# A list scheduler's latency table: result latency between dependent operations of one engine, and extra latency into TensorE

## The chip, the cores and the metric

The kernel runs on one core of one Trainium2 chip. The metric is the device time of one execution in microseconds (us); smaller is better. The times shown are those of three plain runs, and one more execution was taken with the hardware profiler. TensorE is called PE, VectorE DVE, ScalarE ACT, GpSimd POOL, and SP is the engine that issues the DMAs.

## The reference

Four layers follow one another on x (2048 tokens of 512 values, bf16): attention with a carried memory, a gated feed-forward network (FFN), the same attention again, the same FFN again. Each is added to its input, and each works on the layer-normalised input. Attention walks over 64 segments of 32 tokens; each segment needs the memory that the one before left:

```python
for s in range(n_seg):                                   # 64 segments of 32 tokens
    h = jnp.concatenate([mem, xs], axis=1)               # 8 memory rows + 32 tokens = 40 rows
    q, k, v = (jnp.einsum('btd,dhe->bhte', h, W) for W in (Wq, Wk, Wv))   # 32 heads of 128
    scores = jnp.where(mask, jnp.einsum('bhqe,bhke->bhqk', q, k) * scale, -1e9)
    o = jnp.einsum('bhqk,bhke->bhqe', softmax(scores), v)
    o = jnp.einsum('bhte,hed->btd', o, Wo)
    mem = o[:, :M, :]                                    # the memory of the next segment
    outs.append(o[:, M:, :])
# FFN:
h = sigmoid(x @ w_gate) * (x @ w_up)                     # 512 -> 1792
y = h @ w_down                                           # 1792 -> 512
```

## The kernel before

**Steps.** The two attention layers run interleaved. Step t (0 to 69) works on segment t of the first layer and, from step 6, on segment t-6 of the second ("both" steps, 6 to 63, have 80 columns, 40 of each). After every fourth step one FFN block of 128 tokens of each layer becomes possible. The serial path is the memory: the output projection of step t must be complete, over all 32 heads, before the first q/k matmul of step t+1.

**One step** (`emit_step`) takes the heads in six groups, five of six heads and a last one of two; they are called groups 0 to 5 here. For each group PE computes q and k in two units of three heads (L385, into one of three PSUM tiles `pj`), ACT copies them to `qku` (L599), and PE computes the scores (L403) into the one PSUM tile `s_ps`. The softmax is a chain of small operations on 104x240 values: DVE adds the mask (L410, `st<-s_ps,maskb`), takes the maximum (L413, `mx`), subtracts it (L415), ACT takes the exponential (L418), DVE sums (L420, `sm`), takes the reciprocal (L422, `rs`) and multiplies twice, once for each layer (L426, `pb`). PE transposes the result (L436, `pt_ps`), ACT or DVE copies it (`ptsb`, L599 or L601), PE multiplies with v (L461, `ot_ps`; v itself comes from L451 and ACT's copy `vsb`), ACT copies (`otsb`), and PE adds the output projection into `wo_ps` (L477). At the end of a step DVE copies the new memory from `wo_ps` into the next step's `hT` (L488).

**The FFN** of a block (`ffn`) uses one PSUM tile, `misc_ps`, for everything: transposes (L510, L324), seven pairs of gate and up products (L535; ACT's tanh L542 and DVE's L544 follow each pair), and fourteen matmuls down (L556). The layer norms (L312 to L318) are chains of four small DVE operations, one POOL operation and one ACT operation.

**What sets the order.** Every piece of work is entered as a `Task` with an engine, a duration in ns and the tiles it reads (`r`) and writes (`w`). `Planner.plan` then runs a list schedule over all tasks of the program: each task has a `tail`, the longest path of durations and latencies to the end; whenever an engine comes free, it takes the ready task with the longest tail. The engines' instruction streams are written in that order, and on the chip every engine works its stream in order. So the table `LAT` never appears as an instruction; it only decides the order. Two successors are told apart: between tasks of one engine the latency is 0, otherwise it is that of the earlier task's engine. The tasks for `ptsb` and for part of `hT` may go to ACT or DVE, whichever the planner finds free first.

Of the kernel before, what the change touches and what calls it, by code (L numbers as in the profile page):

```python
# [12 lines left out]
ALU = mybir.AluOpType  # L13
# [10 lines left out]
EPS = 1e-5  # L24
# [18 lines left out]
class Task:  # L43
    __slots__ = ("eng", "dur", "lat", "fn", "deps", "succ", "tail", "boost", "ndep", "ready", "start", "idx", "on")

    def __init__(self, eng, dur, lat, fn, boost):
        self.eng, self.dur, self.lat, self.fn, self.boost = eng, dur, lat, fn, boost
        self.deps, self.succ = set(), []


class Planner:

    LAT = {"PE": 215.0, "DVE": 130.0, "ACT": 140.0, "POOL": 450.0, "SP": 2200.0}

# [5 lines left out]
    def add(self, eng, dur, fn, r=(), w=(), lat=None, boost=0.0):  # L62
        engs = eng if isinstance(eng, tuple) else (eng,)
        tk = Task(engs, dur, self.LAT[engs[0]] if lat is None else lat, fn, boost)
        tk.idx = len(self.tasks)
        for k in r:
            if k in self.writer:
                tk.deps.add(self.writer[k])
        for k in w:
            if k in self.writer:  # L70
                tk.deps.add(self.writer[k])
            for q in self.readers.get(k, ()):
                tk.deps.add(q)
# [7 lines left out]
        return tk  # L81

    def plan(self):
        T = self.tasks
# [17 lines left out]
        ready = {e: [] for e in free}  # L102
# [11 lines left out]
        while left:  # L114
            best = None
            for e in free:
# [5 lines left out]
                if h:  # L122
                    t = free[e]
# [6 lines left out]
            t, e = best  # L130
# [24 lines left out]
class Kern:  # L155
# [149 lines left out]
    def layernorm_T(self, xb, xkey):  # L305
# [6 lines left out]
        pl.add("DVE", dve_ns(D), lambda: nc.vector.bn_stats(out=ln[:, 0:6], in_=xb), r=[xkey], w=[lk])  # L312
        pl.add("DVE", 100, lambda: nc.vector.bn_aggr(out=ln[:, 6:8], in_=ln[:, 0:6]), w=[lk])
        pl.add("DVE", 80, lambda: nc.vector.tensor_scalar(out=ln[:, 8:9], in0=ln[:, 7:8], scalar1=EPS, scalar2=None, op0=ALU.add), w=[lk])
        pl.add("POOL", 500, lambda: nc.gpsimd.tensor_tensor(out=ln[:, 9:10], in0=ln[:, 8:9], in1=self.negh[:], op=ALU.pow), w=[lk], lat=100)
        pl.add("DVE", 80, lambda: nc.vector.scalar_tensor_tensor(out=ln[:, 10:11], in0=ln[:, 6:7], scalar=-1.0, in1=ln[:, 9:10],
                                                                  op0=ALU.mult, op1=ALU.mult), w=[lk])
        pl.add("ACT", act_ns(D) + 180, lambda: nc.scalar.activation(out=xn[:], in_=xb, func=ACTF.Identity, bias=ln[:, 10:11], scale=ln[:, 9:10]),  # L318
# [27 lines left out]
    def emit_step(self, t):  # L346
# [21 lines left out]
        for g, (h0, gsz, us) in enumerate(self.groups):  # L368
            hs = slice(0, gsz)
            for u in us:  # L370
# [29 lines left out]
                def sc(uh=uh, nh=nh, qku=qku, h0=h0):  # L400
# [19 lines left out]
            pl.add("DVE", dve_ns(n), lambda hs=hs, st=st, sm=sm: nc.vector.tensor_reduce(out=sm[pr, hs], in_=st[pr, hs], axis=AX.X, op=ALU.add),  # L420
# [238 lines left out]
```

## Time and profile before

| | |
|---|---|
| median of the three runs | 2194.81 us (2194.67 to 2200.37) |
| the profiled execution's own time | 2198.24 us |
| its span, first to last instruction | 2196.4 us |
| PE busy | 2056.8 us, 42116 matmuls |
| ACT busy | 1299.0 us |
| DVE busy | 1270.8 us |
| granted PE clock, mean | 0.987 |

A page of the profile gives busy times, a chain of waits followed back from the last instruction, groups of instructions, and DMA issues. A row of a timeline reads: start, duration, engine, line, operation, output<-inputs, how many were merged, and in brackets how long the engine sat idle before it and for whom. A row of a windows view gives, for a stretch of time, its length and the busy time and instruction count of PE, PE's weight loads (PEld), DVE, ACT and POOL, then the granted PE clock, the busy share of the DMA engines and their GB/s. A matmul's recorded duration includes the time in the pipeline, so matmuls overlap in the records; what a matmul costs PE is the distance from one start to the next, and the rows of the chain of waits give just that.

### The profile page before, as it was taken

The numbers are of one execution on the slowest core, as the hardware profiler recorded it, in microseconds if no ns is written. First come the engines' busy times: TensorE is split into PE (matmuls) and PEld (weight loads), VectorE is DVE, ScalarE is ACT, GpSimd is POOL, SyncE is SP. The second block draws the span as 40 slices with busy tenths as digits, with TensorE's granted clock in tenths as the row PEclk, the third lists the DMA queues.
The fourth block names the chain that finished last, engine by engine and source line by source line (L and its number), as shares of the span: only waits on it lengthen the run. The fifth ranks groups of instructions, "written<-read, shape, count | busy, mean of one in ns | idle before, by whom it ended". The sixth has DMA issues, their size and how long they took to land.

```text
span 2196.4 us, 93329 instructions
## 1 busy us (share of the span) xinstructions
PE 2056.8 (94%) x42116; PEld 1742.8 (79%) x42116; DVE 1270.8 (58%) x3743; ACT 1299.0 (59%) x2919; POOL 43.5 (2%) x77
## 2 busy tenths in 40 slices
PE   4999999999999999999999999999999999999996
PEld 3777878788887878888787778878787888878775
DVE  4566566556646655665566466556655655565653
ACT  3556566565656656565666556566665666666552
POOL 1000000000000000000000000000000000000000
PEclk8999999999999999999999999999999999999997
DMA  9030223233232323324132332423233242324223
GB/s 333 29 89 17 77 60 108 74 108 103 75 108 60 108 74 108 103 75 122 55 113 60 108 103 74 119 58 109 63 113 98 83 116 60 115 58 126 70 61 107
DMA packets 317330, 203.17 MB, mean 92 GB/s; under 512 B 11770, under 2 KB 316930, under 8 KB 316930
## 3 DMA queue, kind: packets, MB, share of 16 engines
q1 hardware_dynamic: 316930, 197.19, 30.7%
q8 instruction: 329, 5.39, 1.0%
q14 instruction: 71, 0.58, 0.1%
HBM read 195.04 MB, written 2.10 MB: 90 GB/s over the span
## 4 chain that ended last, share of the span: by engine, by line
PE 62%; DVE 29%; issue 3%; ACT 3%; DMA 2%; POOL 0%; DVEq 0%; POOLq 0%; ACTq 0%
PE pj L385 22%; PE pj L451 16%; PE misc_ps L535 7%; PE wo_ps L477 7%; DVE pb L426 7%; DVE st L410 4%; DVE mx L413 3%; DVE st L415 3%; DVE sm L420 3%; PE misc_ps L556 3%; PE s_ps L403 3%; DVE ptsb L601 2%; DMA wd<-in_B_w_down_dram 2%; PE ot_ps L461 2%; PE pt_ps L436 2%
## 5 line engine op out<-in xcount | busy, mean ns | idle before, releaser
L385 PE MATMUL pj<-hT,wq_sb 128*128 128x80 bf16 (+1 forms) x8960 | 626.4, 198 | 16.1 <-DVE hT L488 13.6
L385 PE MATMUL pj<-hT,wk_sb 128*128 128x80 bf16 (+1 forms) x8960 | 627.6, 198 | 0.0
L451 PE MATMUL pj<-wv_sb,hT 128*104 128x512 bf16 x2240 | 568.3, 384 | 1.8 <-ACT vsb L599 1.6
L385 PEld LDWEIGHTS <-wq_sb 128*128 128x128 bf16 x8960 | 465.2, 99 | 59.6 <-issue 21.7
L599 ACT CAST qku<-pj 128x480 bf16<-128x480 f32 (+3 forms) x770 | 389.4, 514 | 144.4 <-PE pj L385 103.9
L599 ACT CAST vsb<-pj 104x512 bf16<-104x512 f32 (+2 forms) x560 | 326.1, 585 | 229.4 <-PE pj L451 223.4
L385 PEld LDWEIGHTS <-wk_sb 128*128 128x128 bf16 x8960 | 451.1, 99 | 0.0
L477 PE MATMUL wo_ps<-otsb,wo_sb 128*128 128x80 bf16 (+1 forms) x8960 | 389.3, 198 | 4.6 <-ACT otsb L599 4.2
L477 PEld LDWEIGHTS <-wo_sb 128*128 128x128 bf16 x8960 | 351.2, 99 | 40.7 <-issue 9.3
L451 PEld LDWEIGHTS <-hT 128*104 128x104 bf16 x2240 | 253.3, 128 | 128.1 <-issue 5.1
L410 DVE TENSOR_TENSOR st<-s_ps,maskb 104x240 f32<-104x240 f32 (+5 forms) x420 | 158.0, 376 | 296.7 <-PE s_ps L403 290.0
L426 DVE TENSOR_TENSOR pb<-st,rs 64x240 bf16<-64x240 f32 (+3 forms) x768 | 287.9, 375 | 26.7 <-DVE rs L422 0.5
L418 ACT ACTIVATE st<-st 104x240 f32<-104x240 f32 (+5 forms) x420 | 161.2, 384 | 188.2 <-DVE st L415 185.7
L599 ACT CAST otsb<-ot_ps 128x480 bf16<-128x480 f32 (+3 forms) x420 | 204.4, 487 | 66.6 <-PE ot_ps L461 60.4
L403 PEld LDWEIGHTS <-qku 128*128 128x128 bf16 x4096 | 173.1, 96 | 78.6 <-issue 34.5
L403 PE MATMUL s_ps<-qku 128*128 128x40 bf16 x4096 | 201.6, 180 | 24.5 <-DVE st L410 21.7
L544 DVE SCALAR_TENSOR_TENSOR hff<-th,misc_ps 128x256 bf16<-128x256 f32 x224 | 93.4, 417 | 210.6 <-ACT th L542 208.9
L420 DVE TENSOR_REDUCE sm<-st 104x6 f32<-104x240 f32 (+5 forms) x420 | 155.8, 371 | 95.7 <-ACT st L418 92.9
L535 PE MATMUL misc_ps<-xnT,wg 128*128 128x128 bf16 x1792 | 176.3, 222 | 9.5 <-DVE hff L544 6.6
L535 PE MATMUL misc_ps<-xnT,wu 128*128 128x128 bf16 x1792 | 176.6, 222 | 0.0
L436 PE MATMUL pt_ps<-ident,pb 128*128 128x80 bf16 (+1 forms) x2240 | 145.4, 198 | 32.8 <-DVE pb L426 27.8
L413 DVE TENSOR_REDUCE mx<-st 104x6 f32<-104x240 f32 (+5 forms) x420 | 156.9, 374 | 13.5
(52 smaller groups left out, 1671.3 us busy)
## 6 DMA issues: line engine op xcount, KB each, us to landing
wg<-in_B_w_gate_dram SPq DMA_DIRECT2D x224, 256.0 KB, 3.1
wu<-in_B_w_up_dram SPq DMA_DIRECT2D x224, 256.0 KB, 3.5
wd<-in_B_w_down_dram SPq DMA_DIRECT2D x224, 256.0 KB, 2.9
wv_sb<-in_A_Wv_dram SPq DMA_DIRECT2D x8, 512.0 KB, 9.6
wo_sb<-in_A_Wo_dram SPq DMA_DIRECT2D x8, 512.0 KB, 8.1
wq_sb<-in_A_Wq_dram SPq DMA_DIRECT2D x5, 768.0 KB, 10.3
wk_sb<-in_A_Wk_dram SPq DMA_DIRECT2D x5, 768.0 KB, 11.1
xs<-in_A_x_dram SPq DMA_DIRECT2D x16, 128.0 KB, 2.1
```

What stands on the lines that cost most here:

```text
L385: nc.tensor.matmul(o_ap, lhsT=W[:, c, h * P:(h + 1) * P], rhs=mv(c), start=(c == 0), stop=(c == DC - 1))
L403: nc.tensor.matmul(s_all[:, uh - h0 + i, :], lhsT=qku[:, i, j, :], rhs=qku[:, i, 2 + j, JOFF * j:JOFF * j + L], start=(idx == 0), stop=(id ...
L410: pl.add("DVE", dve_ns(n, True), lambda gsz=gsz, hs=hs, st=st: nc.vector.tensor_tensor(out=st[pr, hs], in0=s_all[pr, hs], in1=self.maskb[p ...
L413: pl.add("DVE", dve_ns(n), lambda hs=hs, st=st, mx=mx: nc.vector.tensor_reduce(out=mx[pr, hs], in_=st[pr, hs], axis=AX.X, op=ALU.max), r=[ ...
L418: pl.add("ACT", act_ns(n), lambda hs=hs, st=st: nc.scalar.activation(out=st[pr, hs], in_=st[pr, hs], func=ACTF.Exp, scale=self.scale), w=[ ...
L420: pl.add("DVE", dve_ns(n), lambda hs=hs, st=st, sm=sm: nc.vector.tensor_reduce(out=sm[pr, hs], in_=st[pr, hs], axis=AX.X, op=ALU.add), r=[ ...
L426: pl.add("DVE", dve_ns(n), lambda gsz=gsz, hs=hs, st=st, rs=rs, pb=pb, pj_=pj_, npj_=npj_, j=j: nc.vector.tensor_tensor(out=pb[pj_, hs, JO ...
L436: nc.tensor.matmul(o_ap, lhsT=pb[:, hl, :], rhs=idn, start=True, stop=True)
L451: nc.tensor.matmul(pv[0:LW, :], lhsT=hT[:, c, :], rhs=self.wv[:, c, n0 * P:(n0 + 4) * P], start=(c == 0), stop=(c == DC - 1))
L477: nc.tensor.matmul(self.wo_ps[:, c * ncol:(c + 1) * ncol], lhsT=self.wo[:, h, c * P:(c + 1) * P], rhs=otsb[:, hl, 0:ncol], start=(h == 0 a ...
L535: nc.tensor.matmul(gu[:, 2 * i + k, :], lhsT=W[:, c, i * P:(i + 1) * P], rhs=xnT[:, c, :], start=(c == 0), stop=(c == DC - 1))
L599: nc.scalar.copy(out=dst, in_=src)
```

## The change

It touches only what the planner believes. Four things are altered:

- `LAT` gets new values, and 45 ns (`TO_PE`) are added wherever the later task is on PE.
- A task now keeps, in `fresh`, those of its dependences that it reads (not those it only overwrites). Between two tasks of DVE, or two of ACT, a `fresh` dependence now costs the latency of the table; it cost 0.
- To make such reads visible, the layer norm's and softmax's in-place tasks now name in `r` the tile that they read.
- The POOL task `pow` is entered with 520 ns and the table's 100 ns, where it had 500 and an explicit 100.

```diff
-    LAT = {"PE": 215.0, "DVE": 130.0, "ACT": 140.0, "POOL": 450.0, "SP": 2200.0}
+    LAT = {"PE": 205.0, "DVE": 122.0, "ACT": 130.0, "POOL": 100.0, "SP": 2200.0}
+    TO_PE = 45.0
...
         for k in r:
             if k in self.writer:
                 tk.deps.add(self.writer[k])
+                tk.fresh.add(self.writer[k])
...
+    def gap(self, a, b):
+
+        if a.eng == b.eng:
+            return a.lat if a.idx in b.fresh and a.eng[0] in ("DVE", "ACT") else 0.0
+        return a.lat + (self.TO_PE if b.eng[0] == "PE" else 0.0)
...
             for s in tk.succ:
-                same = T[s].eng == tk.eng
-                m = max(m, T[s].tail + (0.0 if same else tk.lat))
+                m = max(m, T[s].tail + self.gap(tk, T[s]))
...
                 n = T[s]
-                same = n.eng == (e,)
-                n.ready = max(n.ready, t + tk.dur + (0.0 if same else tk.lat))
+                n.ready = max(n.ready, t + tk.dur + self.gap(tk, n))
...
-        pl.add("DVE", 100, lambda: nc.vector.bn_aggr(out=ln[:, 6:8], in_=ln[:, 0:6]), w=[lk])
+        pl.add("DVE", 100, lambda: nc.vector.bn_aggr(out=ln[:, 6:8], in_=ln[:, 0:6]), r=[lk], w=[lk])
...
                 out=st[pr, hs], in0=st[pr, hs], in1=mx[pr, hs].unsqueeze(2).to_broadcast([npart, gsz, L]), op=ALU.subtract),
-                r=[("mx", gi)], w=[("st", gi)])
+                r=[("mx", gi), ("st", gi)], w=[("st", gi)])
             pl.add("ACT", act_ns(n), lambda hs=hs, st=st: nc.scalar.activation(out=st[pr, hs], in_=st[pr, hs], func=ACTF.Exp, scale=self.scale),
-                   w=[("st", gi)])
+                   r=[("st", gi)], w=[("st", gi)])
```

No instruction is added, removed or altered in itself; PE has the same 42116 matmuls. The order of nearly every engine's stream changes somewhere, and 41 of the 420 copies to `ptsb` go from DVE to ACT (170 on DVE before, 129 now). The line numbers of the changed kernel are larger by 6 from `Kern` on: L410 is L416 there, L601 is L607, and so on.

The first place is DVE's stream in the middle of step 30. Before, from the mask addition of group 2 (`st_77<-s_ps`) to that of group 3 (`st_78<-s_ps`):

```order
L410 TENSOR_TENSOR st_77<-s_ps,maskb 104x240
L413 TENSOR_REDUCE mx_81<-st_77 104x6
L415 TENSOR_TENSOR st_77<-st_77,mx_81 104x240
L420 TENSOR_REDUCE sm_84<-st_78 104x6
L422 RECIPROCAL rs_86<-sm_84 104x6
L426 TENSOR_TENSOR pb_80<-st_78,rs_86 64x6x40
L426 TENSOR_TENSOR pb_80<-st_78,rs_86 40x6x40
L420 TENSOR_REDUCE sm_83<-st_77 104x6
L422 RECIPROCAL rs_85<-sm_83 104x6
L426 TENSOR_TENSOR pb_79<-st_77,rs_85 64x6x40
L426 TENSOR_TENSOR pb_79<-st_77,rs_85 40x6x40
L410 TENSOR_TENSOR st_78<-s_ps,maskb 104x240
```

The same place in the changed kernel (`st_77` is again group 2, `st_78` first group 1 and, from its next mask addition on, group 3):

```order
L416 TENSOR_TENSOR st_77<-s_ps,maskb 104x240
L428 RECIPROCAL rs_86<-sm_84 104x6
L607 CAST ptsb_87<-pt_ps 128x480
L419 TENSOR_REDUCE mx_81<-st_77 104x6
L432 TENSOR_TENSOR pb_80<-st_78,rs_86 64x6x40
L421 TENSOR_TENSOR st_77<-st_77,mx_81 104x240
L432 TENSOR_TENSOR pb_80<-st_78,rs_86 40x6x40
L426 TENSOR_REDUCE sm_83<-st_77 104x6
L416 TENSOR_TENSOR st_78<-s_ps,maskb 104x240
L428 RECIPROCAL rs_85<-sm_83 104x6
L522 TENSOR_TENSOR xa_99<-misc_ps,xs_93 128x512
L419 TENSOR_REDUCE mx_82<-st_78 104x6
```

Before, an operation was followed by the one that reads its result nearly everywhere; now operations of two groups alternate, and the mask addition of group 3 stands ahead of group 2's reciprocal and multiplications, where it stood behind them. Over the whole program, 1787 neighbouring pairs of DVE's stream were dependent ones, and 1109 are now.

The second place is PE's stream at the end of step 28: the last output projections and what follows them. Before:

```order
L477 LDWEIGHTS wo_sb
L477 MATMUL wo_ps<-otsb_91,wo_sb 128x80
L477 LDWEIGHTS wo_sb
L477 MATMUL wo_ps<-otsb_91,wo_sb 128x80
L385 LDWEIGHTS wq_sb
L385 MATMUL pj_128<-hT_70,wq_sb 128x80
```

At the same six positions now:

```order
L541 LDWEIGHTS wu_114
L541 MATMUL misc_ps<-xnT_107,wu_114 128x128
L541 LDWEIGHTS wu_114
L541 MATMUL misc_ps<-xnT_107,wu_114 128x128
L391 LDWEIGHTS wq_sb
L391 MATMUL pj_128<-hT_70,wq_sb 128x80
```

Eight matmuls of the FFN (four of `wg`, four of `wu`) now stand between the last projection of the step and the first q/k matmul of the next; they stood ahead of that projection. In steps 8 to 61 the order repeats every four steps. Of four step ends there, one had an FFN piece at this position before (two matmuls of L556), and three have now: eight matmuls after step 28, sixteen after step 30, and the two of L556 after step 31, as before. Step 29 has none.

A third displacement is on PE between score pieces. Before, scores of a group's two units had up to a q/k piece between them; now they are mostly neighbours. From the last score matmul of group 3 to the first of group 4 there stood, in steps 28 to 31, pieces of 0.65 to 0.88 us; now there stand pieces of 1.08 to 1.52 us, worked out from the row counts and the distance of starts of each shape in the trace of before.

More of the change, by code (lines that the diff above doesn't have):

```diff
@@ L43 @@
 class Task:
-    __slots__ = ("eng", "dur", "lat", "fn", "deps", "succ", "tail", "boost", "ndep", "ready", "start", "idx", "on")
+    __slots__ = ("eng", "dur", "lat", "fn", "deps", "succ", "tail", "boost", "ndep", "ready", "start", "idx", "on", "fresh")
     def __init__(self, eng, dur, lat, fn, boost):
         self.eng, self.dur, self.lat, self.fn, self.boost = eng, dur, lat, fn, boost
-        self.deps, self.succ = set(), []
+        self.deps, self.succ, self.fresh = set(), [], set()
 class Planner:
-    LAT = {"PE": 215.0, "DVE": 130.0, "ACT": 140.0, "POOL": 450.0, "SP": 2200.0}
+    LAT = {"PE": 205.0, "DVE": 122.0, "ACT": 130.0, "POOL": 100.0, "SP": 2200.0}
+    TO_PE = 45.0
     def __init__(self):
```

6 lines of the change are left out of this document (3 added, 3 removed).

## The prediction

> **What bounds the kernel now.** I read the page first: its engine shares and the chain that ended last.
>
> ```profile
> span 2196.4 us, 93329 instructions
> PE 2056.8 (94%) x42116; PEld 1742.8 (79%) x42116; DVE 1270.8 (58%) x3743; ACT 1299.0 (59%) x2919; POOL 43.5 (2%) x77
> PE 62%; DVE 29%; issue 3%; ACT 3%; DMA 2%; POOL 0%; DVEq 0%; POOLq 0%; ACTq 0%
> ```
>
> PE is busy nearly all the time, yet 29% of the chain is DVE, which is busy only 58%. So DVE decides in certain places. A table of stages shows where; the row of 126.60 us is one repeat of four steps (28 to 31), the last row is the crowded middle of step 30.
>
> ```profile
> 0.00:57.00 57.00, 28.46 (x524) 21.90 (x525) 22.56 (x62) 18.28 (x44) 9.47 (x15) 0.83 1.04 332
> 230.00:1949.00 1719.00, 1645.38 (x33110) 1405.45 (x33110) 1016.74 (x2981) 1044.94 (x2281) 29.11 (x53) 1.00 0.32 91
> 2134.00:2196.40 62.40, 45.90 (x712) 34.47 (x709) 19.81 (x56) 18.94 (x49) 0.55 (x1) 0.74 0.40 116
> 866.40:993.00 126.60, 121.73 (x2454) 104.03 (x2452) 75.32 (x221) 77.20 (x169) 2.20 (x4) 1.00 0.32 92
> 944.00:954.00 10.00, 8.94 (x167) 7.17 (x165) 9.34 (x29) 7.66 (x16) 0.55 (x1) 1.00 0.01 2
> ```
>
> The steady part is 1719 us, so it matters most; it is 13.6 repeats of 126.6 us, of which steps 8 to 61 are 13.5. In the crowded middle DVE is at 93% and ACT at 77%: there DVE is the bound.
>
> What PE must do in four steps follows from the code's counts and the distance of starts, which the chain of waits gives (start, us, engine, output, line, count):
>
> ```profile
> 869.66 0.86 PE pj L385 x24
> 889.48 1.73 PE pj L451 x8
> 882.49 0.31 PE s_ps L403 x12
> 891.21 0.86 PE wo_ps L477 x24
> 893.03 0.45 PE misc_ps L535 x8
> 892.16 0.22 PE pt_ps L436 x6
> 868.36 0.43 PE misc_ps L556 x2
> 876.39 0.22 PE misc_ps L324 x4
> ```
>
> 1024 q/k matmuls cost 36.7 us, 128 of v 27.7, 256 scores 6.6, 512 projections 18.3, 224 gate/up 12.6, 256 transposes and products with v 9.4, 28 down 6.0, 24 of the norms 1.3: together 118.6 us. So **PE loses 8.0 of 126.6 us** in each repeat, and no order can gain more than about 13.5 x 8.0 = 108 us there. PE's waits in this window name most of it (us in total, times, longest):
>
> ```profile
> PE s_ps L403 <- DVE st L410: 1.5, 2, 1.1
> PE pj L385 <- DVE hT L488: 0.9, 3, 0.3
> PE misc_ps L324 <- ACT xn L318: 0.9, 1, 0.9
> PE pt_ps L436 <- DVE pb L426: 0.8, 2, 0.6
> ```
>
> They show less than is lost, because each matmul's record runs on in the pipeline. Step 30 shows how much: six matmuls from 945.91 would let the next start at 946.12; it starts at 947.35, so 1.23 us are lost where the bracket says 1.06.
>
> ```profile
> 945.17 0.46 PE L403 MATMUL s_ps<-qku 128*128 128x40 bf16 x12
> 945.91 0.38 PE L461 MATMUL ot_ps<-ptsb,vsb 128*128 128x80 bf16 x6
> 947.35 0.30 PE L403 MATMUL s_ps<-qku 128*128 128x40 bf16 x6 [1.06 <-DVE st L410]
> ```
>
> The cause is on DVE:
>
> ```profile
> 942.60 0.40 DVE L410 TENSOR_TENSOR st<-s_ps,maskb 104x240 f32<-104x240 f32 x1
> 943.03 0.40 DVE L413 TENSOR_REDUCE mx<-st 104x6 f32<-104x240 f32 x1
> 943.47 0.41 DVE L415 TENSOR_TENSOR st<-st,mx 104x240 f32<-104x240 f32 x1
> 943.80 0.40 DVE L420 TENSOR_REDUCE sm<-st 104x6 f32<-104x240 f32 x1
> 944.23 0.19 DVE L422 RECIPROCAL rs<-sm 104x6 f32<-104x6 f32 x1
> 945.30 0.40 DVE L420 TENSOR_REDUCE sm<-st 104x6 f32<-104x240 f32 x1
> 945.74 0.19 DVE L422 RECIPROCAL rs<-sm 104x6 f32<-104x6 f32 x1
> 946.04 0.82 DVE L426 TENSOR_TENSOR pb<-st,rs 64x240 bf16<-64x240 f32 x2
> 946.89 0.41 DVE L410 TENSOR_TENSOR st<-s_ps,maskb 104x240 f32<-104x240 f32 x1
> 947.21 0.41 DVE L516 TENSOR_TENSOR xa<-misc_ps,xs 128x512 bf16<-128x512 bf16 x1
> ```
>
> Group 3's scores are done at 945.48, but its mask addition (946.89) stands in the queue behind group 2's sum, reciprocal and multiplications. And the distances of starts tell the price that the old table left out: an operation that reads its forerunner's result starts 0.43 to 0.44 us after it (942.60, 943.03, 943.47; 943.80 to 944.23), one that doesn't 0.32 to 0.33 (943.47 to 943.80; 946.89 to 947.21). The **0.11 us** between them is what the new 122 ns stands for. The old plan believed each softmax chain some 0.5 us shorter than it is, so PE's pieces were put where their inputs aren't ready.
>
> The Trainium skill speaks against this gain: "VectorE: DVE Perf Modes", section "The DRAIN you can't avoid", says that the next DVE operation starts only when the pipe is empty, whether or not a semaphore stands between, so that independent neighbours would save nothing. The trace decides otherwise here, by 0.32 against 0.44 us; the same section allows an earlier start for an operation that isn't held.
>
> **The change part by part**, per repeat of four steps. No instruction's duration changes; each term is a wait.
>
> (a) *Step ends.* Today three of the four step ends cost PE 0.48 us each:
>
> ```profile
> 959.40 0.45 PE L477 MATMUL wo_ps<-otsb,wo_sb 128*128 128x80 bf16 x8
> 960.17 0.30 PE L385 MATMUL pj<-hT,wq_sb 128*128 128x80 bf16 x4 [0.31 <-DVE hT L488]
> ```
>
> (eight projections from 959.40 end at 959.69; 960.17 is 0.48 later.) The new order puts 0.45 us of FFN into one of them and 0.90 into another. Saved: 0.45 + 0.48 = **0.9 us**. Bounds: 0, if these FFN pieces themselves wait for `misc_ps`, to 1.4.
>
> (b) *Scores waiting for `s_ps`.* Over the program the page names 21.7 us:
>
> ```profile
> L403 PE MATMUL s_ps<-qku 128*128 128x40 bf16 x4096 | 201.6, 180 | 24.5 <-DVE st L410 21.7
> ```
>
> In the repeat it is the 1.5 us of the row above, 0.17 more for each of its two waits, and 0.4 in two waits too short to open a gap between records (counted from starts): 2.2 us, all before group 4's scores. Now 1.1 to 1.5 us of PE work stands there in place of 0.65 to 0.88, and in step 30 the mask addition stands ahead of the three operations that it waited for, which took 945.74 to 946.86. The piece needs group 3's scores, DVE free, and 0.46 us (946.89 to 947.35). I expect 0.3 us to be left and take **1.9**. Bounds: 0.8 (group 3's addition late in every step as today's step 30) to 2.2.
>
> (c) *Transposes waiting for `pb`.* Today 1.65 us: 0.8 in the row, 0.17 for each of its two, and 0.5 in short ones. For groups 0 to 4 the work between scores and transposes is now 4.8 to 8.6 us, and the chain takes 4 to 5.5 when I lay step 30's new DVE order on the distances above. For the small group 5 only 3.2 to 3.5 us stand there, and in steps 29 and 30 layer-norm operations cut in: some 0.4 and 0.7 us of wait. Saved: **0.4**. Bounds: -1.0 to 1.65.
>
> (d) *The second layer's norm in step 29.*
>
> ```profile
> 921.11 0.60 PE L556 MATMUL misc_ps<-wd,hff 128*128 128x512 bf16 x2
> 926.56 0.40 PE L324 MATMUL misc_ps<-ident,xn 128*128 128x128 bf16 x4 [0.88 <-ACT xn L318]
> ```
>
> From the last down product (end 921.55) to the transposes it takes 5.0 us, with 4.0 us of PE work between; now 4.4 us stands there. That is 1.05 us (0.88 and the hidden 0.17); the next transposes wait 0.3. Of these 1.35 I take 0.8 as left: **0.55** saved. Bounds: 0 to 1.35.
>
> (e) *Small waits* on `ptsb`, `otsb` and `hff`, 1.2 us together (8.0 less 1.4, 2.2, 1.65, 1.35 and 0.2 of DMA). In step 29 the last projection now follows its own product with v at once, which costs some 0.5; others go. Saved: **0.35**. Bounds: -0.6 to 1.2.
>
> The sum is 0.9 + 1.9 + 0.4 + 0.55 + 0.35 = 4.1 us per repeat, half of what is lost; 13.5 repeats give **55 us**. Outside them I take nothing: the first 57 us wait for weights (DMA share 1.04) and PE's clock (0.83); the last 62 are the last FFN block alone, whose order is the same. In steps 0 to 7 and 62 to 69 five step ends lose the FFN piece that they had (5 x 0.45 = 2.2 us), against smaller waits in the other terms; bounds -5 to +10 us. The profiled execution took 2198.24 us, 1.8 more than its span; 2198.2 - 55 = 2143, and it lay 3.4 us above the runs' median of 2194.81, so I predict **2139 us**.
>
> **The rivals.**
>
> *Only PE's own distances help.* What stands against my walk through DVE is that a chain cut by other operations gets longer: each inserted operation costs 0.32 where it saves 0.11. Term (a) stays 0.9. Term (b), with group 3 ready as late as today (1.0 to 1.9 us after its scores; 945.48 to 947.35 is the longest) against 1.1 to 1.5 us of work now, leaves 0.7: 1.5 saved. The transposes of group 3 come 5.1 to 6.2 us after its scores today, against 4.8 to 5.7 us of work now, and lose 0.6; the rest stays. 1.8 us per repeat, 24 in all: 2171 us. By the rule of the Trainium skill weighed above this would be the outcome; the 0.11 us of this trace speak against it.
>
> *The waits only move.* Every wait removed from `s_ps` comes back at transposes and norms; (b) and (c) at their lower ends, (d) 0, (e) -0.6, (a) 0.45: 0.35 us lost per repeat, 5 us in all: 2200 us, inside what is called no change below.
>
> *ACT becomes the late engine: slower.*
>
> ```profile
> L599 ACT CAST ptsb<-pt_ps 128x480 bf16<-128x480 f32 (+2 forms) x250 | 117.1, 469 | 70.6 <-PE pt_ps L436 67.2 <-DVE st L410 1.3 <-DVE sm L420 0.4
> ```
>
> 41 such copies move to ACT, three net in each repeat, and they gather in the crowded middle: in step 28 groups 1, 2 and 3 change from DVE to ACT. ACT is at 77% there, so about five more copies of 0.47 us fill the ten us; from that point the `qku` copies behind them are late, `pj` stays full, and PE waits. Two such waits of 0.47 in each step cost 3.8 us per repeat; with only (a) gained that is 2.9 x 13.5 = 39 us slower: 2234 us. Against it: at most three more per step, and the exponentials beside them come earlier.
>
> **How the numbers follow.** Chances: forecast 0.70 (2105 to 2160), distances only 0.14, moved waits 0.07, ACT late 0.09. With every term at its upper end, 8.0 less 0.2 of DMA waits is gone, about 100 us; I don't believe that of step 29, whose end has no piece and whose last projection waits (1.0 us stays), and with half a microsecond left in each of the other steps it is 6.3 x 13.5 = 85 us: 2110. The range reaches from a little below that, 2108, to 2186, past the first rival; it leaves out the two last rivals and a little at the lower end. A measurement of this kernel tells 0.3% (6.6 us) from no change: faster by more 0.84, within 0.07, slower by more 0.09.
>
> **What would show it.** In the profile after: a repeat of about 122.5 us with the same 118.6 of PE work; three PE waits on `hT` per repeat gone down to one; the wait of `s_ps` on L416 down from 21.7 us over the program to below 6; `pt_ps` on `pb` little smaller. Wrong would be a growing wait of `qku` or `pj` on ACT, FFN pieces at the step ends that wait for `hff`, or neighbours on DVE that start 0.44 us apart though independent.

## The result and the profile after

| | before | after |
|---|---|---|
| median of four runs each, side by side on one chip | 2194.74 us (2193.3 to 2200.37) | 2104.16 us (2100.89 to 2105.69) |
| the profiled execution | 2198.24 us | 2105.36 us |

The ratio is 0.9581 with a 95% interval of 0.956 to 0.9602: the changed kernel is 90.6 us (4.2%) faster. The forecast was 55 us, to 2139. The direction holds, and so does the mechanism at the step ends and the scores; the size doesn't, and the time lies 4 us below the range's lower end.

The page of the changed kernel, with the lines that were read first in the one of before (span, busy times, shares of the chain that ended last):

```profile
span 2103.6 us, 93419 instructions
PE 2021.3 (96%) x42006; PEld 1735.4 (82%) x42116; DVE 1197.1 (57%) x3702; ACT 1304.5 (62%) x2960; POOL 43.8 (2%) x77
PE 82%; DVE 10%; ACT 3%; issue 2%; DMA 1%; another core or an unknown queue 0%; POOL 0%; ACTq 0%; SPq 0%; POOLq 0%; DVEq 0%
```

DVE's part of the chain falls from 29% to 10%, though its share of busy time only goes from 58 to 57%: DVE holds PE back in far fewer places. (110 records of L562's matmuls are missing, 42006 for 42116, so PE's busy time and counts are a little low here; starts and spans are not touched by that.)

The stages of the changed kernel, at the same points of the program as the table in the prediction (stretch, length, busy time and count of PE, PEld, DVE, ACT and POOL, granted clock, DMA share, GB/s):

```profile
0.00:57.00 57.00, 28.06 (x495) 21.18 (x496) 22.84 (x62) 18.45 (x44) 9.52 (x15) 0.82 1.04 332
223.00:1863.00 1640.00, 1615.62 (x33009) 1398.40 (x33102) 953.39 (x2939) 1048.23 (x2323) 29.12 (x53) 1.00 0.33 96
2042.00:2103.60 61.60, 44.50 (x687) 33.73 (x691) 19.45 (x56) 19.12 (x49) 0.55 (x1) 0.72 0.39 113
830.60:951.90 121.30, 119.61 (x2446) 103.56 (x2453) 70.66 (x219) 77.67 (x173) 2.20 (x4) 1.00 0.34 96
905.50:915.50 10.00, 9.78 (x213) 8.42 (x211) 9.61 (x32) 7.49 (x17) 0.55 (x1) 1.00 0.02 4
```

Put beside the rows of before, this says where the 92.8 us of span went. Both tables cut off the first 57 us alike. From 57 to the start of the steady part it took 230 - 57 = 173 us and takes 223 - 57 = 166: 7 us. The steady part went from 1719 to 1640: **79 us**, 5.3 in each repeat (126.6 to 121.3). From its end to the last block it took 2134 - 1949 = 185 and takes 2042 - 1863 = 179: 6 us. The last block gives 0.8. So 14 us came from the edges, where the forecast had nothing. In the crowded middle PE is now busy 9.78 of 10 us, where it was 8.94, while DVE is busier than before (96%, was 93): both engines are nearly full there now, and more work passes.

PE's waits in steps 28 to 31 (us in total, times, longest), which were four groups with 4.1 us:

```profile
PE wo_ps L483 <- ACT otsb L605: 0.6, 2, 0.4
PE pj L391 <- DVE hT L494: 0.3, 1, 0.3
PE misc_ps L330 <- ACT xn L324: 0.2, 1, 0.2
```

Scores waiting for `s_ps` are gone, and over the whole program no such wait is long enough to show; transposes still wait (the idle time stands behind the bar, with those who ended it):

```profile
L409 PE MATMUL s_ps<-qku 128*128 128x40 bf16 x4096 | 182.5, 180 | 1.5 <-ACT qku L605 0.8 <-ACT vsb L605 0.7
L442 PE MATMUL pt_ps<-ident,pb 128*128 128x80 bf16 (+1 forms) x2240 | 145.0, 197 | 16.8 <-DVE pb L432 12.4 <-DVE ptsb L607 2.0 <-DVE lns L320 0.9
L483 PE MATMUL wo_ps<-otsb,wo_sb 128*128 128x80 bf16 (+1 forms) x8960 | 392.4, 198 | 10.6 <-ACT otsb L605 9.3
```

The scores' row had 24.5 us of idle time, 21.7 of it for DVE's mask addition; none of that is left.

The middle of step 30 shows how. DVE's timeline in the changed kernel:

```profile
904.03 0.40 DVE L426 TENSOR_REDUCE sm<-st 104x6 f32<-104x240 f32 x1 [0.47 <-ACT st L424]
904.35 0.40 DVE L416 TENSOR_TENSOR st<-s_ps,maskb 104x240 f32<-104x240 f32 x1
904.66 0.18 DVE L428 RECIPROCAL rs<-sm 104x6 f32<-104x6 f32 x1
904.76 0.61 DVE L607 CAST ptsb<-pt_ps 128x480 bf16<-128x480 f32 x1
905.29 0.39 DVE L419 TENSOR_REDUCE mx<-st 104x6 f32<-104x240 f32 x1
905.60 0.39 DVE L432 TENSOR_TENSOR pb<-st,rs 64x240 bf16<-64x240 f32 x1
905.92 0.39 DVE L421 TENSOR_TENSOR st<-st,mx 104x240 f32<-104x240 f32 x1
906.34 0.41 DVE L432 TENSOR_TENSOR pb<-st,rs 40x240 bf16<-40x240 f32 x1
906.78 0.40 DVE L426 TENSOR_REDUCE sm<-st 104x6 f32<-104x240 f32 x1
907.10 0.40 DVE L416 TENSOR_TENSOR st<-s_ps,maskb 104x240 f32<-104x240 f32 x1
907.41 0.18 DVE L428 RECIPROCAL rs<-sm 104x6 f32<-104x6 f32 x1
```

and PE's around it:

```profile
906.48 0.46 PE L409 MATMUL s_ps<-qku 128*128 128x40 bf16 x12
906.80 0.39 PE L442 MATMUL pt_ps<-ident,pb 128*128 128x80 bf16 x6
...
908.34 0.46 PE L409 MATMUL s_ps<-qku 128*128 128x40 bf16 x12
```

Operations of two groups alternate, and most starts lie 0.31 or 0.32 us apart (904.03 to 904.35 to 904.66, 905.29 to 905.60 to 905.92, 906.78 to 907.10 to 907.41); two are farther apart (905.92 to 906.34 to 906.78). Between these two stands the second layer's multiplication (`pb`, 40x240), which works on partitions 64 to 103. In both kernels, in steps 8 to 61, it starts 0.40 to 0.43 us after a softmax operation on 240 columns and the next operation 0.43 to 0.44 us after it (where DVE isn't idle between), though neither reads the other; so mixing gains nothing at these places. Group 3's scores are done at 906.80, its mask addition starts 0.30 us later, where it took 1.41 (945.48 to 946.89), and group 4's scores at 908.34 find `s_ps` long free.

### The profile page after: what moved, and what is told of

Read it like the earlier page. It is cut to its first block, busy times and chain, and to the rows that moved or that the text cites. A ratio compares the mean times of both kernels' runs of the same rounds, so it can differ in the third digit from the quotient of the medians.

```text
span 2103.6 us, 93419 instructions
## 1 busy us (share of the span) xinstructions
PE 2021.3 (96%) x42006; PEld 1735.4 (82%) x42116; DVE 1197.1 (57%) x3702; ACT 1304.5 (62%) x2960; POOL 43.8 (2%) x77
## 4 chain that ended last, share of the span: by engine, by line
PE 82%; DVE 10%; ACT 3%; issue 2%; DMA 1%; another core or an unknown queue 0%; POOL 0%; ACTq 0%; SPq 0%; POOLq 0%; DVEq 0%
PE pj L391 27%; PE pj L457 20%; PE wo_ps L483 11%; PE misc_ps L541 10%; PE s_ps L409 4%; PE misc_ps L562 3%; PE ot_ps L467 3%; PE pt_ps L442 3%; DVE pb L432 2%; DVE sm L426 1%; DVE st L416 1%; DVE mx L419 1%; DMA wd<-in_B_w_down_dram 1%; DVE ptsb L607 1%; ACT otsb L605 1%
## 5 line engine op out<-in xcount | busy, mean ns | idle before, releaser
L391 PEld LDWEIGHTS <-wq_sb 128*128 128x128 bf16 x8960 | 472.1, 99 | 69.1 <-issue 13.8
L605 ACT CAST qku<-pj 128x480 bf16<-128x480 f32 (+3 forms) x770 | 380.3, 515 | 185.2 <-PE pj L391 161.9
L483 PE MATMUL wo_ps<-otsb,wo_sb 128*128 128x80 bf16 (+1 forms) x8960 | 392.4, 198 | 10.6 <-ACT otsb L605 9.3
L416 DVE TENSOR_TENSOR st<-s_ps,maskb 104x240 f32<-104x240 f32 (+5 forms) x420 | 157.3, 375 | 280.0 <-PE s_ps L409 276.5
L605 ACT CAST ptsb<-pt_ps 128x480 bf16<-128x480 f32 (+3 forms) x291 | 138.7, 477 | 74.6 <-PE pt_ps L442 72.3
L409 PE MATMUL s_ps<-qku 128*128 128x40 bf16 x4096 | 182.5, 180 | 1.5 <-ACT qku L605 0.8
L421 DVE TENSOR_TENSOR st<-st,mx 104x240 f32<-104x240 f32 (+5 forms) x420 | 158.3, 377 | 9.6
L409 PEld LDWEIGHTS <-qku 128*128 128x128 bf16 x4096 | 150.7, 96 | 14.8 <-issue 1.9
```

What stands on the lines that cost most here:

```text
L391: nc.tensor.matmul(o_ap, lhsT=W[:, c, h * P:(h + 1) * P], rhs=mv(c), start=(c == 0), stop=(c == DC - 1))
L409: nc.tensor.matmul(s_all[:, uh - h0 + i, :], lhsT=qku[:, i, j, :], rhs=qku[:, i, 2 + j, JOFF * j:JOFF * j + L], start=(idx == 0), stop=(id ...
L416: pl.add("DVE", dve_ns(n, True), lambda gsz=gsz, hs=hs, st=st: nc.vector.tensor_tensor(out=st[pr, hs], in0=s_all[pr, hs], in1=self.maskb[p ...
L421: pl.add("DVE", dve_ns(n), lambda gsz=gsz, hs=hs, st=st, mx=mx: nc.vector.tensor_tensor(out=st[pr, hs], in0=st[pr, hs], in1=mx[pr, hs].uns ...
L483: nc.tensor.matmul(self.wo_ps[:, c * ncol:(c + 1) * ncol], lhsT=self.wo[:, h, c * P:(c + 1) * P], rhs=otsb[:, hl, 0:ncol], start=(h == 0 a ...
L605: nc.scalar.copy(out=dst, in_=src)
```

## The experiments

Each kernel was timed against the one before in rounds; the four batches had medians of 2195.4, 2197.3, 2196.7 and 2198.2 us for that kernel. Medians and ratios with 95% intervals (gains and losses in the text are counted against the median of the same batch, the change's gain being 90.6):

| kernel | us | ratio |
|---|---|---|
| the change | 2104.16 | 0.9581 (0.956 to 0.9602) |
| e1: only same-engine latency | 2111.54 | 0.9613 (0.9597 to 0.9629) |
| e2: only 45 ns into PE | 2187.07 | 0.9959 (0.9944 to 0.9974) |
| e3: only the new `LAT` | 2172.37 | 0.9892 (0.9878 to 0.9907) |
| e4: the change without the 45 ns | 2107.38 | 0.9596 (0.9582 to 0.9611) |
| e7: no FFN at step ends | 2125.81 | 0.9673 (0.9658 to 0.9687) |
| e5: new order, old engine of each copy | 2137.82 | 0.9733 (0.9717 to 0.9749) |
| e6: old order, new engine of each copy | 2208.42 | 1.0057 (1.004 to 1.0074) |
| e8: same-engine latency in the softmax only | 2111.04 | 0.9605 (0.9591 to 0.9619) |
| e9: same-engine latency in the norms only | 2171.87 | 0.9882 (0.9867 to 0.9897) |
| e12: DVE's dependent operations put together again | 2178.73 | 0.9924 (0.9909 to 0.9939) |
| e13: same order, pads on DVE | 2165.43 | 0.9852 (0.9835 to 0.9868) |
| e10: same-engine latency halved | 2120.33 | 0.9653 (0.9638 to 0.9667) |
| e11: same-engine latency doubled | 2092.55 | 0.9526 (0.9512 to 0.954) |
| e14: same-engine latency tripled | 2093.27 | 0.9526 (0.9512 to 0.954) |

Where PE's losses are given below "by starts", they are counted from the trace: the distance from one matmul's start to the next, less the distance that its shape has where nothing waits, summed over steps 8 to 61 by the line of the later matmul. Before, these losses are 122.8 us; in the changed kernel, 44.3.

### Which of the three numbers does it

e1 takes only the latency between dependent tasks of one engine, with the old values:

```diff
-    LAT = {"PE": 205.0, "DVE": 122.0, "ACT": 130.0, "POOL": 100.0, "SP": 2200.0}
-    TO_PE = 45.0
+    LAT = {"PE": 215.0, "DVE": 130.0, "ACT": 140.0, "POOL": 100.0, "SP": 2200.0}
+    TO_PE = 0.0
```

> The old latency values, no 45 ns into PE, only the new latency between dependent operations of one engine (DVE, ACT). Its order has 1220 dependent neighbours on DVE (1787 before, 1109 with the whole change), the score pieces stand as far apart as with the whole change, but the end of step 28 has no FFN piece. Theory 'chain length' (the gain comes from planning the softmax chains at their real length): 2104 plus 0.45 x 13.5 = 6 us, 2105 to 2118 us. Theory 'into PE' (the 45 ns carry it): 2165 to 2195 us. Theory 'any numbers' (a reshuffle that happened to be good): anywhere, 2130 to 2200 us.

e2 takes only the 45 ns, e3 only the new values; in both, `gap` is as before inside an engine:

```diff
         if a.eng == b.eng:
-            return a.lat if a.idx in b.fresh and a.eng[0] in ("DVE", "ACT") else 0.0
+            return 0.0
```

> Only the 45 ns into PE, old latency values, nothing between operations of one engine. 1750 dependent neighbours on DVE; three of four step ends have an FFN piece, as with the whole change; in two of the four steps the scores of group 4 stand as close to group 3's as before. 'Chain length': the step ends (0.9 us per repeat, 12 us) and about half of the scores' waits (1.2 us, 16 us) go: 2160 to 2180 us. 'Into PE': 2104 to 2125 us.

> Only the new values of the table (205, 122, 130); no 45 ns, nothing between operations of one engine. 1829 dependent neighbours on DVE, distances between score pieces as before but in one step. 'Chain length' and 'into PE': 2180 to 2205 us, no gain. 'Any numbers': a change of more than 15 us in either direction.

e4 is the change with `TO_PE = 0.0`:

> The whole change without the 45 ns into PE. 1171 dependent neighbours on DVE, score pieces as with the whole change, one FFN piece less at the step ends. 'Chain length': 2105 to 2118 us, as in e1. 'Into PE': 2165 to 2195 us.

e1 gives 84 of the 91 us, and e4 with the new values 88: the same-engine latency is the change. What the 45 ns add to it (2107.4 to 2104.2) is 3 us, and the two intervals overlap, so that this is anything is not shown. e2 missed both expectations: it gained 8 us, not the 15 to 35 that the one theory named nor the 70 and more of the other. PE's largest waits in e2, over the program:

```profile
PE pt_ps L442 <- DVE pb L432: 31.2, 69, 2.9
...
PE s_ps L409 <- DVE st L416: 15.3, 43, 0.9
```

The scores' wait fell from 21.7 to 15.3, the transposes' grew from 27.8 to 31.2. By starts the step ends went from 19.6 to 7.2 us, just as in the full change, but the transposes from 22.7 to 29.3 and L461's from 6.6 to 9.9: a gain at one place given back at two others.

e3 missed what two of the theories said of it (no gain) and went the way of the third, "any numbers": it gained 23 us (by starts the second norm's wait went from 18.9 to 5.8, the scores' from 29.7 to 21.3). The new values lower what a dependence costs; that such a reshuffle by itself is worth 1% means that an effect of that size can't be put down to a planner's number being truer. e1 with 84 us is far above it.

### Softmax or norms

e8 and e9 have e1's values, with `fresh` kept for one of the two only:

```diff
-                tk.fresh.add(self.writer[k])
+                if k[0] != "lns":
+                    tk.fresh.add(self.writer[k])
```

(e9 has `==`.)

> As e1 (old values, no 45 ns), but the new latency between dependent operations counts only where the tile read isn't the layer norm's; so the softmax chains have their length and the norms don't. 'Softmax chain length': 2112 us of e1 plus what the norm's waits cost before (18.9 us on L324 against 4.2 in e1): 2112 to 2127 us, with the scores' wait at 0. If the norms mattered most: above 2150 us.

> The counterpart of e8: only the layer norm's chains have the new latency. 1744 dependent neighbours on DVE. 'Softmax chain length': only L324's wait goes, 10 to 15 us, as e3 also showed: 2175 to 2195 us, with the scores' wait above 20 us. If the norms mattered most: below 2150 us.

The softmax alone gives all of it (86 us; e1 gives 84), the norms alone 25, and the two don't add. e8 came out a little below its expected interval, because the norms' wait fell there too, to 3.5 us by starts, although the norms were planned as before: once the softmax has its places, the norms have theirs. In the other direction it works only in part: e9's trace still names 11.6 us at the scores and 23.3 at the transposes. e9 missed its expectation (2175 to 2195 us, with more than 20 us at the scores) by 3 us, and its 25 us are hardly more than the 23 of e3, which changes no such latency; that they come from the norms' planning isn't shown.

For the softmax the other kernels speak against a lucky reshuffle: the six that plan its same-engine latency and are built as planned (e1, e4, e8 and, below, e10, e11, e14) lie between 2093 and 2120 us, the three that don't (e2, e3, e9) between 2172 and 2187.

### What carries it: PE's pieces at better distances, or a faster DVE

The prediction had both: mixed neighbours on DVE start 0.11 us earlier, and PE has more work between a group's scores and what waits for them. e12 keeps PE's order and every other engine's, but moves on DVE the reader of a result up behind its forerunner where nothing between is needed for it:

```diff
+                    if A.idx in B.fresh:
+                        if seen and not B.deps & {k.idx for k in order[seen[0]:p]}:
+                            order[seen[0]:p + 1] = [B] + order[seen[0]:p]
...
-        order = self.pl.plan()
+        order = self.runs(self.pl.plan())
```

(A loop over the order with A the DVE task at hand, B the next ones, and `seen` those between, at most two.) Dependent neighbours are 1861 then, where the changed kernel has 1109.

> The whole change with PE's, ACT's and all engines' own choices kept, but on DVE an operation that reads its forerunner's result is moved up behind it wherever nothing that it needs stands between: 1861 dependent neighbours on DVE (1109 with the change, 1787 before). 'Distances' (what matters is where PE's pieces stand; how DVE mixes its chains does not): 2104 to 2112 us. 'Mixing' (0.11 us saved at each independent neighbour in the crowded middle): 750 x 0.11 = 83 us more of DVE time, a third to a half of it where DVE decides: 2130 to 2146 us.

73 of the 91 us are gone, more than either theory had named (2104 to 2112 us for distances alone, 2130 to 2146 for mixing). e12 also delays what stood between, so e13 leaves the order as it is and puts at the same places an operation that nothing reads:

```diff
+        self.pad = c.tile([P, 96], F32, name="pad")
...
+                            tk = Task(("DVE",), 0.0, 0.0, lambda: self.nc.vector.memset(self.pad[:], 0.0), 0.0)
+                            tk.on = "DVE"
+                            out.append(tk)
```

It only adds 871 unused clears of 128x96 between the others.

> The whole change, order kept, with 871 small memsets of an unused tile (128x96 f32) put on DVE, one behind each operation whose reader stands one or two places further on. Each takes about the 0.11 us that an independent neighbour saves, so DVE loses the time won by mixing (871 x 0.11 = 96 us of DVE time) but no operation of one chain stands behind another chain's run, as in e12. 'Rate' (mixing pays because DVE gets 0.11 us per neighbour): 2150 to 2180 us, near e12. 'Queue order' (mixing pays because a chain doesn't wait for another chain's run): 2104 to 2120 us.

58 us are gone, at an unchanged order, inside the 2150 to 2180 us of "rate". DVE's timeline in e13 has the price of a pad:

```profile
927.67 0.34 DVE L427 TENSOR_REDUCE sm<-st 104x6 f32<-104x240 f32 x1
927.99 0.14 DVE L606 MEMSET pad<- 128x96 f32 x1
928.04 0.34 DVE L422 TENSOR_TENSOR st<-st,mx 104x240 f32<-104x240 f32 x1
...
929.37 0.40 DVE L427 TENSOR_REDUCE sm<-st 104x6 f32<-104x240 f32 x1
929.74 0.14 DVE L606 MEMSET pad<- 128x96 f32 x1
929.79 0.10 DVE L321 TENSOR_SCALAR lns<-lns 128x1 f32<-128x1 f32 x1
```

The next operation starts 0.37 and 0.42 us after the sum, where it would start 0.32: a pad takes 0.05 to 0.10 us here. Over the 679 pads with no idle time beside them whose two neighbours also follow each other in the changed kernel it is 0.09 us in the mean, a little less than what a dependent neighbour costs. PE's first waits are, in e12,

```profile
PE pt_ps L442 <- DVE pb L432: 27.8, 67, 2.9
PE misc_ps L330 <- ACT xn L324: 14.3, 31, 3.4
PE pt_ps L442 <- DVE ptsb L627: 11.0, 17, 1.5
```

and in e13,

```profile
PE pt_ps L443 <- DVE pb L433: 18.0, 30, 2.9
PE misc_ps L331 <- ACT xn L325: 11.6, 30, 3.4
PE pt_ps L443 <- DVE ptsb L629: 9.1, 8, 2.1
```

In both the transposes and the norms are late again. The scores are not: by starts e12 loses 1.4 us at them, where the kernel before loses 29.7. So two gains are told apart: **the scores' wait is cured by the new order's distances, even at the old rate of DVE; the transposes' and norms' need DVE's rate.** The edges go with DVE, too, as the distances between the first q/k matmuls of steps 0, 8 and 62 and the last matmul of the program show:

| us | before | the change | e12 | e13 |
|---|---|---|---|---|
| steps 0 to 7 | 216.9 | 209.1 | 216.1 | 212.4 |
| steps 8 to 61 | 1718.4 | 1639.9 | 1698.5 | 1672.5 |
| step 62 to the end | 243.2 | 236.2 | 243.8 | 260.4 |

In steps 8 to 61, then, e12 loses 58.6 us against the change and e13 32.6. e13's last part holds more than DVE's work, as the rows from step 62 to the end show (the changed kernel first, then e13; the granted clock is the third number from the end):

```profile
1863.00:2103.60 240.60, 216.38 (x4688) 180.19 (x4699) 125.56 (x385) 133.07 (x328) 2.94 (x5) 0.93 0.30 86
1899.00:2163.70 264.70, 225.78 (x4700) 185.50 (x4699) 141.16 (x485) 133.22 (x328) 2.90 (x5) 0.90 0.27 78
```

The clock is 0.90 there, where the change has 0.93 and the kernel before 0.94 (1949 us to the end); why, the runs don't show. An estimate from these rows: 0.10 of 265 us less 0.07 of 241, some 10 of the 24 us that e13 loses there.

The rule of the Trainium skill that the prediction weighed ("VectorE: DVE Perf Modes", "The DRAIN you can't avoid") would make dependent neighbours cost DVE no more than others. The trace has 0.43 to 0.44 us for them against 0.31 to 0.33, and e12 loses 73 us with 752 more of them, so the measurement decides against it here.

### The step ends

e7 takes the FFN pieces that the change puts between a step's last projection and the next q/k matmul, and puts the first q/k piece ahead of them:

```diff
+                order[last + 1:i + 1] = stay + [order[i]] + moved
...
-        order = self.pl.plan()
+        order = self.unfill(self.pl.plan())
```

(`moved` are the FFN's tasks there and those that depend on them.)

> The whole change, but at every step end the first q/k piece of the next step is put ahead of the FFN pieces that the planner had placed there; the rest of the order stays. 'Waits add up' (as the prediction summed its terms): the wait on hT rises from 7.2 to about 26 us in steps 8 to 61, and the time by as much: 2104 + 19 = 2123 us. 'Waits overlap' (a wait at one place gives later chains the time that they lacked, so other waits shrink): hT rises as said, the others fall by a third or more of it, 2110 to 2117 us.

It lost 19 of the 91 us, as "waits add up" had it. PE's largest wait in e7 was 5.4 us in the change:

```profile
PE pj L391 <- DVE hT L494: 18.0, 57, 0.3
```

By starts this wait goes from 7.2 to 25.8 us and all others together grow by some 3, so no other wait shrinks in return: a wait at the step end, where all of PE hangs on `hT`, is paid in full.

### The copies that changed engine

The planner also moved 41 copies from DVE to ACT. That is the net: of the 548 tasks that have the choice (these copies and `hT`'s), 219 change their engine. e5 has the changed planner but the engine of each of the 420 copies and of `hT`'s as before; e6 is the reverse (`COPIES` is the list of engines that the other plan chose):

```diff
         order = self.pl.plan()
+        for tk, c in zip([k for k in self.pl.tasks if len(k.eng) == 2], COPIES):
+            tk.on = "ACT" if c == "A" else "DVE"
```

> The whole change's order, but each copy that may go to ACT or DVE (ptsb, part of hT) runs on the engine that the plan of before gave it: 170 of the ptsb copies on DVE again. 'Copies' (the gain comes from 41 copies leaving DVE in the crowded middle): most of the gain goes, 2140 to 2190 us. 'Chain length': the copies cost DVE some 0.56 us each where they fall into a chain, 2106 to 2130 us.

> The counterpart of e5: the order of before, but each copy that may go to ACT or DVE runs where the new plan puts it (129 of the ptsb copies on DVE, 170 before). 'Copies': DVE is relieved in the crowded middle, the waits of scores and transposes fall, 2160 to 2180 us. 'The order and the engines belong together' (a copy helps where it was planned): 2190 to 2215 us.

e5 lies between its two expectations: the order alone keeps 59 us, and 31 depend on the engines of these tasks. PE's two largest waits in e5:

```profile
PE misc_ps L333 <- ACT xn L327: 19.4, 31, 3.4
PE misc_ps L544 <- DVE hff L553: 16.0, 20, 0.9
```

With the copies back on DVE, what DVE does for the FFN and the norms is late. In e6 the new choice is worse than nothing under the old order (12 us slower). The engines of the copies belong to their order.

### Too little and too much latency

e10, e11 and e14 scale the same-engine latency alone (0.5, 2 and 3):

```diff
-            return a.lat if a.idx in b.fresh and a.eng[0] in ("DVE", "ACT") else 0.0
+            return 2.0 * a.lat if a.idx in b.fresh and a.eng[0] in ("DVE", "ACT") else 0.0
```

> The whole change with half the latency (61 and 65 ns) between dependent operations of one engine. 1301 dependent neighbours. 'Chain length': each softmax chain is believed 0.3 us shorter than it is, so some of the waits of transposes and scores come back: 2108 to 2140 us. If only the kind of order mattered, and not the length: 2100 to 2108 us.

> The whole change with twice that latency (244 and 260 ns). 758 dependent neighbours, the last group's transposes 3.9 to 6.1 us behind its scores (3.2 to 3.5 with the change). 'Chain length': chains believed 0.6 us too long, so PE's pieces stand later than they need; waits before transposes vanish, but the step's end comes later and the step ends wait more: 2105 to 2135 us.

> The whole change with three times the latency (366 and 390 ns) between dependent operations of one engine; group 5's transposes stand 5 to 7 us behind its scores. If slack in front of the transposes is all that still pays after e11 (2092.6 us, no wait left there), nothing more is to be had and the step ends wait longer: 2092 to 2115 us. If the mixing itself still pays: below 2090 us.

Half the latency keeps 76 us of the gain, inside the range of "chain length". Twice the latency was expected to lose some, and **beats both kernels**: 2092.55 us, another 12 below the change; three times gives the same, as was expected if nothing more is to be had. Idle time of PE's lines in e11:

```profile
L391 PE MATMUL pj<-hT,wq_sb 128*128 128x80 bf16 (+1 forms) x8960 | 625.1, 198 | 21.9 <-DVE hT L494 17.9 <-DVE hT L499 2.6
L483 PE MATMUL wo_ps<-otsb,wo_sb 128*128 128x80 bf16 (+1 forms) x8960 | 384.6, 198 | 2.1 <-ACT otsb L605 0.2
L442 PE MATMUL pt_ps<-ident,pb 128*128 128x80 bf16 (+1 forms) x2240 | 144.7, 197 | 10.5 <-DVE pb L432 9.3 <-DVE ptsb L607 1.1
```

The projections' idle time falls from 10.6 to 2.1 us and the transposes' from 16.8 to 10.5, at the price of the step ends (`hT` 5.4 to 17.9). Of the 11 us between the two spans 5.7 come from steps 0 to 7 (203.4 us, for 209.1) and 4.3 from steps 8 to 61. Dependent neighbours on DVE fall from 1109 to 758. More than the true latency may act as slack against waits that the planner doesn't model; no run tests this.

## Why the prediction was right in kind and short in size

By starts, over steps 8 to 61 (13.5 repeats):

| term | lost before, us | lost after | saved | forecast (per repeat x 13.5) |
|---|---|---|---|---|
| (a) step ends, `hT` | 19.6 | 7.2 | 12.4 | 12.2 |
| (b) scores, `s_ps` | 29.7 | 0.0 | 29.7 | 25.7 |
| (c) transposes, L436 | 22.7 | 3.6 | 19.1 | 5.4 |
| (d) norm, L324 | 18.9 | 5.4 | 13.5 | 7.4 |
| (e) the rest | 31.9 | 28.1 | 3.8 | 4.7 |
| sum | 122.8 | 44.3 | 78.5 | 55 |
| outside these steps | | | 14.8 | 0 |

Two steps of the prediction failed: (c), where it foresaw 5.4 us and 19.1 were saved, and "Outside them I take nothing", where 14.8 were saved, above its bound of 10. The 78.5 us of steps 8 to 61 alone would have stayed inside the range, which was drawn for up to 85. (The 6.3 us per repeat behind these 85 take off half a microsecond once; half a microsecond in each of three steps would have left 5.3, 72 us in all.)

**(a)** was right, and e7 shows it by undoing it: 19 us, against 18.6 more lost at the step ends by starts.

**(b)** was right in mechanism and nearly in size: the prediction left 0.3 us in each repeat, and none is left. Its reason, longer pieces of PE together with an earlier mask addition in step 30, fits: in e12, which loses only 1.4 us here, group 3's mask addition comes 0.60 to 0.90 us behind its scores in steps 28 to 31, and in step 30 that is 0.90 for 1.41 before. With 1.41 the longest piece, 1.52 us, would not have covered it (1.41 + 0.46 = 1.87). DVE's better rate isn't needed for it.

**(c)** is the term of the sum that failed: "For the small group 5 only 3.2 to 3.5 us stand there, and in steps 29 and 30 layer-norm operations cut in: some 0.4 and 0.7 us of wait. Saved: **0.4**." The chain was sized well; that it ends in a wait was wrong. The end of step 30 in the changed kernel, PE's timeline (the transposes of group 5 are the two matmuls of the last row):

```profile
914.40 0.39 PE L442 MATMUL pt_ps<-ident,pb 128*128 128x80 bf16 x6
...
915.44 0.40 PE L330 MATMUL misc_ps<-ident,xn 128*128 128x128 bf16 x4 [0.22 <-ACT xn L324]
...
917.39 0.23 PE L442 MATMUL pt_ps<-ident,pb 128*128 128x80 bf16 x2
```

and DVE's:

```profile
914.45 0.23 DVE L416 TENSOR_TENSOR st<-s_ps,maskb 104x80 f32<-104x80 f32 x1
...
916.77 0.49 DVE L432 TENSOR_TENSOR pb<-st,rs 64x80 bf16<-64x80 f32 x2
```

From group 5's scores it takes 1.25 us to the mask addition, 2.57 from there to the second multiplication and 0.38 to the transposes, 4.2 us, against 3.47 of PE work between: the 0.7 us of the walk are there. But PE had already been held 0.71 us on the way, by the norm (0.39 by starts, 0.22 in the bracket), L467 (0.20) and group 4's transposes (0.12), so group 5's transposes start with no wait. In step 29 0.16 us was left of the 0.4. Waits on one engine's path lie one behind the other: an earlier one pays for a later one. The prediction counted both, here and in (d).

The other half of (c) is that DVE passes more work where it is the bound. The prediction used the 0.11 us only to explain the order, and walked one step. Without this rate the transposes lose by starts some 32 us (e12) and 20 (e13) in steps 8 to 61, and these steps take 59 and 33 us longer; e12's figure holds the delay of what stood between, so the rate's own share should be nearer to e13's.

**(d)** had the right place, with the size off: 13.5 for 7.4 us. The prediction left 0.8 of 1.35 us in each repeat; 0.39 is left. e8 shows that this doesn't need the norms to be planned otherwise: the softmax's new order alone frees DVE for them.

**(e)** is right in sum for partly wrong reasons. The transfers of `wd`, which the prediction had left out, give 6.5 us (9.4 to 2.9); without them the small waits cost 2.7 more than before. The projection in step 29 behaves as foreseen: 0.59 us a repeat, for "some 0.5".

**"Outside them I take nothing"** failed as well: 7.8 us in steps 0 to 7 and 7.0 from step 62 on, where by starts the transposes gave most (20.1 to 14.3 in the one, 7.6 to 4.7 in the other). The same chains run there, so a gain per step that comes from DVE's rate belongs to all 70 steps. e12 takes it away there, too; e13 takes away more at the end, part of it by the clock.

The rivals. *Only PE's own distances help*, 2171 us, comes nearest to e12, which gives 2178.7: the size was right for a kernel whose DVE neighbours stay dependent. Its premise is true besides: from mask addition to the last multiplication the chains of groups 0 to 2 did get longer (2.88 to 3.34, 3.19 to 3.94, 3.45 to 4.26 us in the mean of steps 8 to 61), and so did group 5's (2.30 to 2.72); only those of groups 3 and 4 got shorter (4.23 to 4.10, 4.48 to 4.19). What it missed is whose chain counts. The transposes of groups 0 to 2 started 2.2 us or more after the last multiplication had, in each group's mean, so there was time to lose (now 1.5 us or more; only group 1 in step 30 has none left, 0.46 us for 0.83). Group 3's started 0.46 us after it in every one of these steps, 0.06 after its end: they always waited, and now 0.78 us lie there on average, 0.59 at least. *The waits only move* happened in e2, not in the change. *ACT becomes the late engine* did not happen: no wait of `pj` on ACT stands among PE's first ones, and with all these tasks back on their old engines (e5) 31 us are lost, not won.

Of the four signs named, three hold: a repeat of 121.3 us (forecast about 122.5), one `hT` wait, no `s_ps` wait. "`pt_ps` on `pb` little smaller" doesn't: 27.8 to 12.4 us. Of the signs of being wrong one was there, in both kernels: independent neighbours on DVE that start 0.40 to 0.44 us apart, wherever the second layer's multiplication is one of the two. The 0.11 us holds for the others.

What stays open: what makes twice the latency better than the true one, and how much of e3's 23 us would come from any other reshuffle.

## What to carry to other kernels

In a list schedule, the distance between dependent operations of one engine belongs in the table as much as the semaphore's: here it alone was worth 4%, and a factor of two too much did better than the exact value. When forecasting, don't add the waits that are left on one engine's path, for an earlier one hides the later ones; and where an engine is nearly full in one stage (DVE at 93% in the middle of a step, 58% on average), count a gain per operation there in every step, the edges included.

## What the runs showed of the hardware

- On DVE an operation on 240 columns starts 0.31 to 0.33 us after an independent neighbour of 104x240 and 0.43 to 0.44 after one whose result it reads. 752 more such dependent neighbours, with the delay of what then stands behind them, cost 73 us (e12).
- The multiplication on partitions 64 to 103 (40x240) starts 0.40 to 0.43 us after a forerunner on 240 columns, and the next operation 0.43 to 0.44 after it, though neither reads the other (both kernels, steps 8 to 61). Where two such multiplications follow each other, in 14 places of e12, the second starts 0.33 us after the first: the longer distance goes with the change of the partitions, not with the operation.
- A small unrelated clear between two DVE operations adds 0.05 to 0.10 us at the places shown and 0.09 in the mean, though its own record is 0.14 us long (e13). 871 of them cost 58 us, 33 of it in steps 8 to 61, for a DVE that is busy 58% of the time.
